# Decode attention beside a gated MLP: K and V loaded by 32 pairs of batch and head and 4 key blocks, in rows of 32 KB

## The chip, the cores and the metric

The kernel runs on one core of one Trainium2 chip. The metric is the time of one execution in microseconds (us), as the device counts it. Three runs of the kernel before took 365.57, 366.02 and 365.81 us; the median is 365.81 us. The profile is of one execution more, with its own span.

## The reference

```python
def _A_ref(x, k_cache, v_cache, wq, wo):        # x 8x1x576, caches 8x16x8192x128
    W = min(4096, max(256, Sk // 4))            # 2048: only the last 2048 keys count
    q = (x @ wq) in 32 heads of 128             # wq 576x4096, two query heads for each K/V head
    scores = q @ k[last W].T * (Dh ** -0.5)
    o = softmax(scores) @ v[last W]
    return o (8 x 4096) @ wo                    # wo 4096x576

def _B_ref(x, w1, b1, w2, b2):
    h = gelu(layernorm(x) @ w1 + b1)            # w1 576x4608
    return h @ w2 + b2                          # w2 4608x576

g = sigmoid((x * gate_w).sum(-1))
out = g * a + (1 - g) * b
```

There are 8 batches of one token each. K and V of the last 2048 keys are 8 x 16 x 2048 x 128 bf16 values each, 67 MB each; with the weights the kernel reads 154 MB once.

## The kernel before

**How the order comes about.** Every piece of work is an op with an engine, a cost, a priority and dependences (`_Plan.add`, `_Plan.dma`). `schedule` (line 62) is a greedy list scheduler: it takes the ready op with the smallest start time less 0.2 us times its priority. What it gives is a fixed order for each engine, and `emit` (line 141) writes the ops in that order with semaphore waits. So an engine never passes an op that waits. The big loads all go out on SyncE's queue (SP), in the order of a list named `stream` (line 571), and each load waits until its slot in SBUF is free.

**The start.** x and the gate come in on ScalarE's queue; wq (4.6 MB) and w1 (5.2 MB) come first on SP's. VectorE makes the layer norm, TensorE the query projection (`q_fn`, line 489) and the first MLP product (`h_fn`, line 524). ScalarE and VectorE make the gelu.

**K and V.** `load_item` (line 600) loads K or V of one K/V head for all 8 batches: 4 MB, as 256 rows of 64 keys by 128 values, that is 16 KB, two rows in each of 128 partitions. There are four slots of 4 MB and a half one. The stream is K0 K1 K2, then V and K in turn, a chunk of wo after every fourth V, and at the end the bias and w2.

**Scores** (`k_unit`, line 639). VectorE transposes K in blocks of 32 x 32 pairs of bf16, half of a load's 2 x 2 pieces at a time (line 647, 128 x 2048 f32), into one of two halves of the tile KT. TensorE then multiplies eight times (line 659, and line 175 for those that keep the weights of the one before), 512 columns each, with a block-diagonal query tile qbd. The results add up in PSUM banks 0 to 3 over the four units of a group of two K/V heads, on top of a mask that ScalarE wrote there (line 629): in each of the 128 rows of scores a quarter of the 2048 columns is that row's batch, and the rest is masked by -1e9.

**Softmax** (line 617), once for each of 8 groups: VectorE takes the maximum over 2048 columns (line 620), a small matmul (line 622) combines the four quarters, ScalarE writes the exponential with its sum (line 624) into the tile P, VectorE transposes P as a whole into PT (line 631), and a small matmul (line 633) gathers the sums.

**The product with V** (`v_item`, line 671). 32 matmuls for each V load (line 681): the weights are 128 x 32 pieces of PT, the moving side is 512 columns of V, in four column positions of the array. At a group's end VectorE picks the valid quarter and sums (lines 691 and 694), GpSimd and TensorE sort it (lines 696 and 700), ScalarE scales it by the gate (line 703) and VectorE transposes it into oT (line 706).

**wo, w2 and the end.** `AccGroup` (line 554) adds products into bank 7, two matmuls of 288 columns for each block of 128 rows (line 563). A wo chunk of 8 blocks is used right after the two groups that it belongs to. After the last V come the bias and w2 in pieces of 12, 12, 8, 3 and 1 blocks. Then two casts (lines 777 and 778) and two stores (line 780).

## Time and profile before

| | before |
|---|---|
| median of 3 runs | 365.81 us (365.57 to 366.02) |
| the profiled execution: span | 364.9 us |
| moved, mean rate over the span | 154.47 MB, 423 GB/s |
| K and V loads | 32 of 4096 KB |
| busy: PE, DVE, ACT, POOL | 247.1, 217.0, 39.9, 23.3 us |
| mean granted TensorE clock | 0.846 |

The profiled execution has no time of its own beside its span; the runs lie 0.7 to 1.1 us above it. The span is counted from the first to the last instruction. PE is TensorE's matmuls, PEld its weight loads, DVE VectorE, ACT ScalarE, POOL GpSimd and SP SyncE. A matmul's row has the duration of one matmul with its drain, and matmuls overlap, so rates are read from the starts. In an answer by windows, each row has the window, its length, the busy time of each engine with the number of instructions, then the granted TensorE clock, the share of the DMA engines and the rate in GB/s. In a timeline, the columns are start, duration, engine, line, operation, output and input, and the count; brackets hold the idle time ahead and what ended it.

### The profile page before, as it was taken

What the parts mean: (1) busy time and instruction counts of PE and PEld (TensorE: products, weight loads), DVE (VectorE), ACT (ScalarE), POOL (GpSimd) and SP (SyncE); (2) the same over time, 40 slices, a digit from 0 to 9 for tenths busy, and PEclk for the clock granted to TensorE, in tenths of its full rate; (3) what the DMA queues carried; (4) which work ended last, traced back from release to release, by engine and by line L of the source; (5) the groups of instructions that cost most, each with busy time, mean ns of one, the idle gap of its engine ahead of it and who ended that gap; (6) DMA issues with size and microseconds to landing.
All of it is one profiled execution on the core that took longest, in us unless ns stands there. A gap on an engine that the chain in (4) does not pass through costs nothing.

```text
span 364.9 us, 2626 instructions
## 1 busy us (share of the span) xinstructions
PE 247.1 (68%) x1347; PEld 57.3 (16%) x893; DVE 217.0 (59%) x160; ACT 39.9 (11%) x46; POOL 23.3 (6%) x66
## 2 busy tenths in 40 slices
PE   0355676599486957849297957868396938587776
PEld 0100000122111121202111121202110210102333
DVE  0723999667883757256675657276756667085220
ACT  1012100400310040000400040000400040001100
POOL 7210001000100000001000100001000100000000
PEclk9986599699769986969768986989589968969699
DMA  8999999999999999999999999999999999999996
GB/s 347 432 408 429 431 433 427 408 429 432 429 431 431 436 427 431 433 431 433 428 431 433 424 433 429 431 435 431 433 429 433 433 431 429 431 431 431 426 428 263
DMA packets 10674, 154.47 MB, mean 423 GB/s; under 512 B 764, under 2 KB 932, under 8 KB 1320
## 3 DMA queue, kind: packets, MB, share of 16 engines
q1 hardware_dynamic: 10608, 154.29, 99.1%
q8 instruction: 8, 0.13, 0.1%
q10 hardware_dynamic: 56, 0.03, 0.0%
q14 instruction: 2, 0.02, 0.0%
HBM read 154.31 MB, written 0.01 MB: 423 GB/s over the span
## 4 chain that ended last, share of the span: by engine, by line
DMA 66%; DVE 21%; PE 10%; issue 1%; ACT 1%; SPq 0%; DVEq 0%
DMA arena<-in_A_k_cache_dram 59%; DVE arena L647 20%; DMA arena<-in_B_w_dram 7%; PE ps L175 5%; PE ps L659 2%; PE ps L681 2%; DVE arena L546 1%; DVE arena L620 1%; ACT ps L629 1%; PE ps L563 0%; DVE arena L545 0%; PE ps L633 0%; DVE arena L777 0%; PE ps L622 0%; SPq L406 0%
## 5 line engine op out<-in xcount | busy, mean ns | idle before, releaser
L647 DVE STREAM_TRANSPOSE arena<-arena 128x2048 f32<-128x2048 f32 x64 | 144.1, 2289 | 61.8 <-DMA arena<-in_A_k_cache_dram 40.6
L175 PE MATMUL ps<-arena 128*128 128x512 bf16 (+2 forms) x454 | 135.0, 449 | 0.0
L659 PE MATMUL ps<-arena 128*128 128x512 bf16 x128 | 57.7, 451 | 52.5 <-DVE arena L647 52.5
L681 PE MATMUL ps<-arena 128*32 128x512 bf16 x512 | 60.3, 390 | 2.6 <-DVE arena L635 1.9
L624 ACT ACTIVATE arena<-ps,arena 128x2048 bf16<-128x2048 f32 x8 | 15.7, 1967 | 240.5 <-DVE arena L623 240.5
L659 PEld LDWEIGHTS ps<-arena 128*128 128x128 bf16 x128 | 14.0, 109 | 171.9 <-DVE arena L647 114.6
L681 PEld LDWEIGHTS ps<-arena 128*32 128x32 bf16 x512 | 25.2, 99 | 46.1 <-issue 20.3
L620 DVE TENSOR_REDUCE arena<-ps 128x1 f32<-128x2048 f32 x8 | 18.3, 2287 | 12.5 <-PE ps L175 12.4
L614 POOL COPY arena<-arena 32x128 bf16<-32x128 bf16 x32 | 9.2, 288 | 211.3 <-PE ps L175 201.5
L631 DVE STREAM_TRANSPOSE arena<-arena 128x2048 bf16<-128x2048 bf16 x8 | 18.3, 2292 | 6.4 <-ACT arena L624 6.4
L691 DVE SCALAR_TENSOR_TENSOR arena<-ps,arena 128x512 f32<-128x512 f32 x8 | 6.0, 751 | 19.8 <-PE ps L681 19.8
L563 PE MATMUL ps<-arena 128*8 128x288 bf16 (+1 forms) x140 | 12.6, 339 | 6.9 <-DVE arena L706 5.6
L700 PE MATMUL ps<-arena 128*128 128x256 f32 x16 | 5.8, 444 | 16.0 <-POOL arena L696 16.0
L633 PE MATMUL ps<-arena 128*128 128x1 f32 x16 | 4.6, 359 | 15.0 <-ACT ps L629 14.2
L629 ACT ACTIVATE ps<-arena 128x2048 f32<-128x2048 f32 x7 | 13.1, 1876 | 0.1
L696 POOL TENSOR_TENSOR arena<-arena 128x256 f32<-128x256 f32 x8 | 4.9, 612 | 111.3 <-DVE arena L623 63.3
L438 PE MATMUL ps<-arena 8*128 8x8 bf16 x8 | 0.6, 171 | 14.7 <-DVE arena L412 9.6
L694 DVE TENSOR_REDUCE arena<-arena 128x128 f32<-128x512 f32 x8 | 8.4, 1048 | 0.3
L563 PEld LDWEIGHTS ps<-arena 128*8 128x8 bf16 (+1 forms) x140 | 6.4, 97 | 13.5 <-DVE arena L706 7.0
L703 ACT ACTIVATE arena<-ps,arena 64x256 bf16<-64x256 f32 x8 | 3.7, 465 | 43.1 <-PE ps L700 43.1
L706 DVE STREAM_TRANSPOSE arena<-arena 128x256 bf16<-128x256 bf16 x4 | 2.5, 634 | 9.8 <-ACT arena L703 9.8
L541 DVE TENSOR_TENSOR arena<-arena 128x1152 f32<-128x1152 f32 x1 | 1.4, 1359 | 10.5 <-ACT arena L539 10.5
(88 smaller groups left out, 66.2 us busy)
## 6 DMA issues: line engine op xcount, KB each, us to landing
arena<-in_A_k_cache_dram SPq DMA_DIRECT2D x16, 4096.0 KB, 28.1
arena<-in_A_v_cache_dram SPq DMA_DIRECT2D x16, 4096.0 KB, 33.0
arena<-in_B_w_dram SPq DMA_DIRECT2D x1, 4608.0 KB, 23.4
arena<-in_A_wo_dram SPq DMA_DIRECT2D x4, 1152.0 KB, 34.7
arena<-in_A_wq_dram SPq DMA_DIRECT2D x1, 4096.0 KB, 13.0
arena<-in_B_w_dram SPq DMA_DIRECT2D x2, 1728.0 KB, 27.3
arena<-in_B_w_dram SPq DMA_DIRECT2D x1, 1152.0 KB, 26.7
arena<-in_B_w_dram SPq DMA_DIRECT2D x1, 576.0 KB, 24.3
```

Source lines behind the costliest of these rows:

```text
L175: return e.add_instruction(mybir.InstMatmult(name=nc.get_next_instruction_name(), engine=mybir.EngineType.PE, ins=[e.lower_ap(rhs), e.lowe ...
L563: ins = e.matmul(ps[32 * j:32 * j + 8, BK_ACC, 0:JN], lhsT, rhs[:, JN * j:JN * j + JN], start=False, stop=True, skip_group_check=True, til ...
L614: return e.tensor_copy(dst, src)
L620: mx = add("dve", lambda e: e.tensor_reduce(out=k(MX), in_=ps[:, 0:4, :].rearrange("p a n -> p (a n)"), axis=AXL.X, op=ALU.max), deps=[qk_ ...
L624: ex = add("act", lambda e: e.activation(out=Pm, in_=ps[:, 0:4, :].rearrange("p a n -> p (a n)"), func=ACTF.Exp, bias=k(NB), scale=SCALE, ...
L629: mask_done[g + 1] = add("act", lambda e: e.activation(out=ps[:, 0:4, :].rearrange("p a (n c) -> p (a n) c", c=4), in_=bass.AP(arena_f, of ...
L631: pt_done[g] = add("dve", lambda e: e.transpose(bass.AP(arena, offset=aoffs("PT") + 2048 * (g % 2), ap=[[AST, 128], [8, 64], [512, 4], [1, ...
L647: tr = add("dve", (lambda h=h, kb=kb: lambda e: e.transpose(bass.AP(arena_f, offset=foffs("KT") + kb * 2048, ap=[[AST // 2, 128], [1, 2048]]),
L659: mm = e.matmul(*args, start=False, stop=True, skip_group_check=True) if rc == 0 else held_matmul(nc, e, *args, stop=True, skip=True)
L681: mm = e.matmul(ps[c:c + 32, BK_OS[g % 2], :], PT[:, g % 2, 16 * c + 32 * t:16 * c + 32 * t + 32], slot(s)[:, (j % 2) * SE + 512 * t:(j % ...
L691: vmul = add("dve", lambda e: e.scalar_tensor_tensor(out=vmv, in0=ps[:, BK_OS[g % 2], :].rearrange("p (r d) -> p r d", r=4), scalar=rr[:, ...
L694: acc_ev[g] = add("dve", lambda e: e.tensor_reduce(out=EV[:, g % 2, :], in_=vm.rearrange("p (r d) -> p d r", r=4), axis=AXL.X, op=ALU.add) ...
```

## The change

A load of K or V now takes 32 pairs of batch and K/V head (two batches) by a quarter of the keys (512): 128 rows, one for each partition, of 128 keys by 128 values, that is 32 KB. There are 4 groups of two batches (NG), and 4 turns of one K and one V load in each (NT), 16 turns in all (NU). The stream is K0 K1 V0 K2 V1 ..., K15 V14 V15, then w2's first 24 blocks, wo in two chunks of 16 blocks, the bias, and w2's last 12.

- **Scores.** As before there are four transposes and 32 matmuls for a K load. Every turn has its own softmax now, 16 instead of 8. The mask leaves one column of eight.
- **Softmax.** The maximum is taken row by row, with no matmul, and the exponential uses it. At a group's end `group_weights` makes from the four maxima and sums of each row the weights by which the four turns are put together.
- **P.** The exponentials are written pair by pair in another order. Four transposes of 32 partitions (`sp`) lay the first half of P into a block-diagonal tile BD, a fifth (`pc`) turns the second half into the tile PC, and ScalarE lays that into BD with four copies of 32 partitions (`sq`). BD is set to zero once, by GpSimd; there is one, so that the spreading of a turn waits for the V product of the turn before (`later`). The last turn uses KT's space instead, which GpSimd sets to zero after the last score.
- **The product with V.** 64 matmuls for each V load, in two halves of 32, each with its own weights of 128 x 128 (every second element of BD's row) and 256 moving columns. VectorE adds the results, weighted, into the tile X, eight operations in a group; two more split X into two bf16 parts, 16 matmuls with the selectors seld sort it, and one VectorE operation scales it into oT.
- **wo** is multiplied after the last group, since every row of it needs all groups.

```diff
-        HG = 2
-        NG = Hkv // HG
+        NB_ = 2
+        NG = B // NB_
+        NT = 4
+        NK = W // (4 * NT)
...
-        WOR = 8
+        WOR = 16
+        WOP = Hq * Dh // 128
...
-        def load_item(cache, nm, hkv):
+        def load_item(which, nm, t):
             s = take_slot()
-            src = cache[:, hkv, S0:Sk, :].rearrange("b (x r) d -> x b (r d)", x=32)
+            g, xq = divmod(t, NT)
+            k0 = S0 + 4 * NK * xq
+            src = ck[which][32 * g:32 * g + 32, k0:k0 + 4 * NK, :].rearrange("i (x r) d -> i x (r d)", x=4)
...
+        def softmax(t):
+            g, x = divmod(t, NT)
+            scores = ps[:, 0:4, :].rearrange("p a n -> p (a n)")
+            mx = add("dve", lambda e: e.tensor_reduce(out=k(g, MX + x), in_=scores, axis=AXL.X, op=ALU.max), deps=[qk_unit[t]], name="mx%d" % t, cost=2.29, prio=5)
+            nb = add("dve", lambda e: e.tensor_scalar(out=k(g, NB + x), in0=k(g, MX + x), scalar1=-SCALE, ...
+            ex = add("act", lambda e: e.activation(out=bass.AP(arena, offset=aoffs("P"), ap=[[AST, 128], [64, 32], [1, 2], [2, 32]]),
+                                                   in_=ps[:, 0:4, :].rearrange("p a (r e c) -> p (a r) e c", e=2, c=32), func=ACTF.Exp, bias=k(g, NB + x), scale=SCALE, accum_out=k(g, S + x)),
+                     deps=[nb] + (p_read[t - 1] if t else [o_zz]), name="exp%d" % t, cost=2.2, prio=5)
...
+            if t + 1 < NU:
+                mask(t + 1, [ex])
...
+            dp = [ex] + bd_zero[home]
+            for a in range(4):
+                def fn(e, a=a):
+                    return e.transpose(bass.AP(arena_f, offset=32 * a * (AST // 2) + foffs(home) + 32 * a, ap=[[AST // 2, 32], [128, 16], [1, 32]]),
+                                       bass.AP(arena_f, offset=32 * a * (AST // 2) + foffs("P"), ap=[[AST // 2, 32], [1, 512]]))
+                sp_done[t][0].append(add("dve", fn, deps=dp, name="sp%d_%d" % (t, a), cost=0.65, prio=5))
+            pc = add("dve", lambda e: e.transpose(view("PC").bitcast(F32), bass.AP(arena_f, offset=foffs("P") + 512, ap=[[AST // 2, 128], [1, 512]])),
+                     deps=[ex] + (sp_done[t - 1][1] if t else []), name="pc%d" % t, cost=0.65, prio=5)
+            for a in range(4):
+                def fn(e, a=a):
+                    return e.activation(out=bass.AP(arena, offset=32 * a * AST + aoffs(home) + 64 * a + 4096, ap=[[AST, 32], [256, 16], [1, 64]]),
+                                        in_=bass.AP(arena, offset=32 * a * AST + aoffs("PC"), ap=[[AST, 32], [64, 16], [1, 64]]), func=ACTF.Copy)
+                sp_done[t][1].append(add("act", fn, deps=[pc] + bd_zero[home], name="sq%d_%d" % (t, a), cost=1.15, prio=3))
+            if x == NT - 1:
+                group_weights(g)
...
+            for v in range(2):
+                def pv_fn(e, v=v):
+                    mm = None
+                    for n in range(NK // 4 * v, NK // 4 * (v + 1)):
+                        q, ee = divmod(n, 2)
+                        mm = e.matmul(dst, bass.AP(arena, offset=aoffs(home) + 256 * q + ee, ap=[[AST, 128], [2, 128]]),
+                                      slot(s).rearrange("p (r k d) -> p r k d", r=2, d=128)[:, :, n, :], start=(n == 0), stop=(n == NK // 2 - 1), skip_group_check=True)
+                    return mm
+                pv = add("pe", pv_fn, deps=[d] + sp_done[t][v] + ([x_read[g - 1]] if g else [o_u]), name="pv%d_%d" % (t, v), cost=4.1, after=pe_hist[-1:])
...
-        M_CUTS = [[12, 12], [8, 3, 1]]
-        stream += [("B", 0)] + [("M", i) for i in range(len(M_CUTS))]
+        M_CUTS = [[24], [8, 3, 1]]
+        stream += [("M", 0), ("W", 0), ("W", 1), ("B", 0), ("M", 1)]
...
+        for t, v, pv in later:
+            for o in sp_done[t][v]:
+                o.deps.append(pv)
```

`group_weights` makes, for each group, small VectorE operations on 1 to 8 columns (`m1`, `mq`, `nm`, `ws`, `ss`, `w8`, `sb`, `rc`, `rg`), one small exponential and two small matmuls; the accumulations into X are named `x`, the split `xh` and `xl`, the sorting `sx` and the scaling `oT`.

In the built program VectorE's fixed order, from the second group on, is this, with `mx` for the maximum and `tr` for a transpose of K. After the `mx` of a group's second turn: `nb`, `tr`, `sp` x4, `pc`, `tr` x3. After that of the third: `nb`, `sp` x4, `pc`, `tr` x4. After that of the fourth: `nb`, `m1`, `mq`, `sp` x4, `pc`, `nm`, `tr` x3, `ws`, `w8`, `x` x4, `ss`, `tr`, `sb`. After that of the next group's first: `nb`, `rc`, `rg`, `tr`, `sp` x4, `pc`, `x` x4, `xh`, `xl`, `tr`, `oT`, `tr` x2. TensorE's order in a turn is four times eight score matmuls, then the two halves of the V product of the turn; after the V product of a group's last turn come two of the next score halves and then `sx`.

## The prediction

> **What bounds the kernel now.** I read the page's slices first, then its chain, then a long window of the loads, then the end of the chain in order of time.
>
> ```profile
> span 364.9 us, 2626 instructions
> ...
> DMA  8999999999999999999999999999999999999996
> GB/s 347 432 408 429 431 433 427 408 429 432 429 431 431 436 427 431 433 431 433 428 431 433 424 433 429 431 435 431 433 429 433 433 431 429 431 431 431 426 428 263
> ...
> DMA 66%; DVE 21%; PE 10%; issue 1%; ACT 1%; SPq 0%; DVEq 0%
> ...
> arena<-in_A_k_cache_dram SPq DMA_DIRECT2D x16, 4096.0 KB, 28.1
> ```
> ```profile
> 40.00:340.00 300.00, 214.68 (x1054) 45.87 (x669) 197.56 (x121) 32.34 (x30) 12.35 (x35) 0.84 1.01 430
> ```
> ```profile
> 334.54 26.68 DMA arena<-in_B_w_dram
> 361.22 0.04 issue
> 361.26 1.73 PE ps L563 x24
> 362.99 0.02 issue
> 363.01 0.45 DVE arena L777
> ```
>
> The DMA engines are full in every slice but the first and last, and the rate stays near 430 GB/s. A K load lands 28.1 us after its issue, although 4096 KB (4.19 MB) at 430 GB/s take 9.75 us: about three loads always stand in the queue. So the loads set the end, and the compute only follows; after the last landing at 361.22 come 3.7 us. What the change does to the time depends on two things: the rate of the loads, and whether the new compute of a turn stays under the 19.5 us that its two loads take.
>
> **The loads.** K and V are 134.2 MB. The second slice holds only wq and w1, whose rows are 32 and 36 KB, at 432 GB/s; K and V at 16 KB run at 430. If 32 KB rows go at 432, they save 134.2/0.430 - 134.2/0.432 = 1.4 us; wo's and w2's longer rows (the slices of 426 and 428) some 0.2 more. No row has 32 KB rows of K, so the bounds are the highest and lowest slice of K and V: at 436 it would be 4.3 us saved, at 408 16.8 us lost. I take 1.6, nearest to the row of like size. Were the loads still the limit, the span would be 363.3 us. The median 365.81 lies 0.9 above the profiled span, so the time would be 364.2.
>
> **The compute of a turn.** These rows price it.
>
> ```profile
> L620 DVE TENSOR_REDUCE arena<-ps 128x1 f32<-128x2048 f32 x8 | 18.3, 2287 | 12.5 <-PE ps L175 12.4
> L631 DVE STREAM_TRANSPOSE arena<-arena 128x2048 bf16<-128x2048 bf16 x8 | 18.3, 2292 | 6.4 <-ACT arena L624 6.4
> L504 DVE STREAM_TRANSPOSE arena<-arena 128x1024 bf16<-128x1024 bf16 x1 | 1.2, 1245 | 0.0
> L624 ACT ACTIVATE arena<-ps,arena 128x2048 bf16<-128x2048 f32 x8 | 15.7, 1967 | 240.5 <-DVE arena L623 240.5
> L624 ACT ACTIVATION_READ_ACCUMULATOR arena<-ps,arena 128x1 f32 x8 | 1.5, 193 | 0.0
> L544 ACT ACTIVATE arena<-arena 128x1152 f32<-128x1152 f32 x1 | 1.2, 1163 | 2.3 <-DVE arena L543 2.3
> L691 DVE SCALAR_TENSOR_TENSOR arena<-ps,arena 128x512 f32<-128x512 f32 x8 | 6.0, 751 | 19.8 <-PE ps L681 19.8
> L541 DVE TENSOR_TENSOR arena<-arena 128x1152 f32<-128x1152 f32 x1 | 1.4, 1359 | 10.5 <-ACT arena L539 10.5
> L420 DVE TENSOR_TENSOR arena<-arena 8x576 f32<-8x576 f32 x1 | 0.7, 747 | 0.0
> L621 DVE TENSOR_SCALAR arena<-arena 128x4 f32<-128x4 f32 x8 | 1.8, 231 | 0.3
> L510 PEld LDWEIGHTS ps<-arena 128*128 128x128 bf16 x4 | 0.3, 98 | 4.0 <-DVE arena L504 3.9
> ```
> ```profile
> 23.18 0.33 PEld L510 LDWEIGHTS ps<-arena 128*128 128x128 bf16 x4 [3.93 <-DVE arena L504]
> 23.19 0.61 PE L510 MATMUL ps<-arena 128*128 128x256 bf16 x4 [2.60 <-DVE arena L504]
> ...
> 276.76 8.89 DVE L647 STREAM_TRANSPOSE arena<-arena 128x2048 f32<-128x2048 f32 x4 [5.69 <-DMA arena<-in_A_k_cache_dram]
> 279.13 0.40 PE L659 MATMUL ps<-arena 128*128 128x512 bf16 x1 [2.76 <-DVE arena L647]
> ...
> 280.04 0.39 PE L659 MATMUL ps<-arena 128*128 128x512 bf16 x1
> ...
> 301.56 0.61 PE L659 MATMUL ps<-arena 128*128 128x512 bf16 x1 [2.47 <-DVE arena L647]
> ...
> 303.25 0.63 PE L659 MATMUL ps<-arena 128*128 128x512 bf16 x1
> ...
> 361.26 1.71 PE L563 MATMUL ps<-arena 128*8 128x288 bf16 x24 [1.11 <-DMA arena<-in_B_w_dram]
> ```
>
> - Transposes of K: 8.89/4 = 2.22 us each. A half of scores, eight matmuls: from 279.13 to 280.04 are four, so 1.82 us, and 0.17 more until its results count (0.40 less 0.23). At the lower clock, 301.56 to 303.25, it is 3.4 us.
> - Maximum 2.29; `nb` 0.2, by the 0.23 of line 621; exponential and its sum 1.97 + 0.19, some 2.1.
> - `sp` and `pc`, five transposes of 512: lines 631 and 504 give 1.02 ns an element and 0.2 us fixed, so 0.72, or 0.65 where they overlap as K's do. I take 0.70, 3.5 us a turn; 32 partitions cost no less than 128 as far as a row shows.
> - `sq`: 1024 elements against 1152 in 1.16 us, so 4.1 us for four. It is on ScalarE beside the first half of the V product and is not in the ring below.
> - The V product: line 510 is nearest, four matmuls of 256 columns, each with its own 128 x 128 weights. Its 0.61 us less one duration of 0.275 is three steps, 0.112 each; 64 make 7.2 us. If the weight loads (0.33/4, 0.08 each) were not hidden, 0.19 each, 12.2 us.
> - The additions `x`, 128 wide: 0.75 us less 384 elements at 1.06 ns (lines 541 and 420) is 0.34.
>
> Where the old kernel could run a group's scores ahead of its softmax, a turn's softmax now stands in a ring with VectorE and TensorE: last half of scores 2.0, maximum 2.3, `nb` 0.2, exponential 2.1, `sp` and `pc` 3.5, then the transposes of the next K. By the built order, after the second turn's maximum one transpose lies beside the exponential and three follow `pc`: 10.1 + 6.7 = 16.8 us. After the third, all four follow: 10.1 + 8.9 = 19.0. After the fourth, four, four `x` and five small operations: 21.3. After the next first, three, four `x`, `xh`, `xl`, `oT` and a wait for `sx`: about 19.6. Together 76.7 us for four turns; their loads at 432 GB/s take 77.7. **At full clock the compute just fits, by 1 us in 78.**
>
> **The clock.** Does TensorE keep it? These windows lie on the steps of the granted clock.
>
> ```profile
> 273.85:277.26 3.41, 2.52 (x14) 0.29 (x4) 0.50 (x1) 0.00 (x0) 0.00 (x0) 1.00 1.02 437
> 277.26:280.67 3.41, 1.54 (x7) 0.19 (x2) 3.41 (x2) 0.00 (x0) 0.00 (x0) 1.00 1.04 447
> ...
> 290.91:294.32 3.41, 1.10 (x8) 0.59 (x4) 1.86 (x3) 1.10 (x1) 0.61 (x1) 1.00 1.05 452
> 294.32:297.73 3.41, 1.61 (x14) 0.71 (x14) 1.93 (x2) 3.31 (x4) 0.00 (x0) 0.50 0.99 423
> 297.73:301.14 3.41, 1.36 (x10) 0.68 (x6) 2.91 (x3) 0.00 (x0) 0.00 (x0) 0.50 1.00 428
> 301.14:304.56 3.42, 3.00 (x8) 0.28 (x3) 2.56 (x2) 0.00 (x0) 0.00 (x0) 0.50 0.99 426
> 304.56:307.97 3.41, 2.81 (x13) 0.27 (x3) 3.00 (x2) 0.00 (x0) 0.00 (x0) 1.00 1.01 428
> ```
>
> A window with 1.54 us of matmuls is followed by full clock, one with 1.10 by half; the clock comes back after a window that is nearly full (3.00). So a step of 3.41 us with over about 2 us idle costs the clock for one or two steps. In the new ring the V product follows the last half of scores and ends 7.2 us on. The first transpose of the next K ends, where it follows `pc`, after 0.2 + 2.3 + 0.2 + 2.1 + 3.5 + 2.2 = 10.5. So TensorE idles 3.3 us after the third turn's scores and some 2.9 after the fourth's (a small matmul stands between); elsewhere the gaps are 1.5 us and less. A gap of 3.1 us has over 2.1 in one step in about 7 of 10 positions. Two such gaps, and a small chance at `sx`, make 1.5 slow spells a group. A spell loses 1.7 us of matmuls for one step, 3.4 for two, less 0.8 that the halves have to spare beside the transposes (2 x 0.4): 0.9 to 2.6, I take 1.75. That is 2.6 us a group, less the margin of 1.0: the compute falls behind by 1.6 us a group, 6.4 in four, and about 2 in the first turns, where the gelu and the slow clock delay it. Before, such spells fell into the wait for K and cost nothing.
>
> **Where the lag shows.** Not in the loads: they are issued two to three ahead, so 8 us of lag empty no queue. It shows at the end, since wo needs every group. Behind K15 come V14, V15, 24 blocks of w2, wo and 12 blocks of w2, 18.4 MB, 42.7 us. The last turn's chain is four transposes 8.9, 2.0, 2.3, 0.2, 2.1, 3.5, `sq` 4.1, half a V product 3.8, two `x` and the split 1.4, `sx` and `oT` 1.7, so 30; w2 matmuls ahead of `sx` add 2.5 and wo 64 x 0.071 = 4.6 us: 37. The transposes of K15 themselves stand behind `sp` and `pc`, some 3 us. That leaves 2.5 us. Of 8.4 us of lag 5.9 are exposed: 363.3 + 5.9 = 369.2 span, **370.0 us**. The other parts cost nothing at this place: GpSimd's zeroing of KT (4096 elements of 4 bytes) lies beside the last maximum and exponential, the mask on ScalarE ends before the first new half can start, and the 16 masks and exponentials with `sq` fill ScalarE to under 9 of 19.4 us. If GpSimd's zeroing were late, each us would add one at the end.
>
> **Rivals.**
> 1. *The clock holds, or its spells cost less than the margin.* Then the loads stay the limit and the time is 364.2, faster than before. For it: the sum fits without spells, and the gap of 2.76 us ahead of 279.13 cost no clock. It decides where the idle part of one step stays under 2 us, or where spells take less than 1.0 us a group and 2.5 at the end. Also here: if longer rows gain nothing, 365.8. The Trainium skill (TensorE: Matmul & The Clock Gate, Part 1) lets the clock fall after an idle window of about 3.4 us; by that rule gaps of 3.3 would mostly keep it. The trace speaks against that rule, since the step from 290.91 was a third busy and the next had half clock.
> 2. *The weight loads of the V product are not hidden.* They are 128 wide now and read every second element. At 12.2 us the next scores start behind the V product, and the ring is 12.2 + 4 x 1.82 + 0.8, about 20.3 us a turn, 14 us more than the loads in 16 turns; less the 2.5 and with no slow spells, 376. Against it: line 510.
> 3. *The new addresses are slower.* Neighbouring rows of a load lay side by side in a batch; now each four do, and the next pair is 2 MB on. Priced by the slice of 408: 364.9 + 16.8 + 0.9 = 382.6, and then the compute has time to spare. No row of before speaks for it. The Trainium skill (DMA: Bandwidth & Descriptors, Latency and other measured facts) reports 207 instead of 214 GB/s for rows 512 KiB apart, 164 at 2 MiB and 103 at 4 MiB. An estimate from its mildest pair, 207/214, would be 10.6 us more; no run here shows it yet.
>
> **How the numbers follow.** The forecast has 0.47; by the bounds of `sp` (0.65 to 0.75, 1 us a group each way), of the spells and of the exposed end, its own range is 366 to 377. Rival 1 has 0.35, rival 2 0.10, rival 3 0.08. About 0.2%, 0.7 us, is what a measurement of this kernel can tell from no change; 365.1 to 366.5 holds 0.04 of rival 1 and 0.03 of the forecast. So faster 0.31, same 0.07, slower 0.62. The range 363.0 to 378.0 leaves out rival 3 and the edges of the others.
>
> **What would show it.** The rate of the slices with K and V near 432 (loads right) or below 425 (rival 3). Starts of the V product's matmuls 0.11 us apart (or 0.19, rival 2). The five transposes near 0.7 us each. The granted clock at 0.5 in some steps behind the third and fourth turns' V products, and the first transpose of a K starting later and later behind its landing, by about 8 us at K15 (if it stays under 4, rival 1). The chain's end on `sx`, `oT` and wo's matmuls instead of a w2 load. I would be wrong if the chain still ends in a load, or if VectorE's transposes wait for K in every turn.

## The result, and the profile after

The changed kernel takes 383.89 us (median of 4 runs, 383.47 to 384.52), beside 365.87 us for the kernel before on the same chip: 1.0495 times as long, 95% interval 1.048 to 1.051. The sign of the forecast was right and its size was not: 370.0 us was said, 13.9 us too little, and the time lies above the range. Of one experiment below (the extra transpose in the held order) three of four runs took 399.76 to 401.66 us at a lower granted clock (0.885 to 0.889 beside 0.913) and are left out, so that a single run of it is used.

The page of the changed kernel, the lines that answer to those of before:

```profile
span 383.0 us, 3868 instructions
...
PEclk9966796989996999996998889898979999898999
...
GB/s 334 469 411 436 435 428 425 421 435 430 438 433 438 438 436 435 429 419 431 435 431 419 405 376 364 431 438 433 404 435 306 421 421 423 421 433 431 411 180 4
...
DVE 51%; PE 24%; ACT 12%; DMA 9%; issue 3%; SPq 0%
...
arena<-in_A_k_cache_dram SPq DMA_DIRECT2D x16, 4096.0 KB, 16.9
```

The chain of work that ended last was 66% loads; now it is 51% VectorE, 24% TensorE and 12% ScalarE. The loads no longer set the end: their rate drops to 376, 364 and 306 GB/s in three slices, the last two hold 180 and 4, and a K load lands 16.9 us after its issue instead of 28.1, so the queue is shorter. The end of the chain, in order of time, is what the forecast said it would be: the last turn's `sq` and V product, then w2, `sx`, `oT` and wo.

```profile
365.82 1.06 ACT arena L654
...
366.92 3.67 PE ps L730 x32
370.59 2.06 PE ps L563 x32
...
374.57 0.45 DVE arena L769
...
375.07 6.01 PE ps L563 x92
```

Next I read what VectorE waited for (the engine and line that wait, what they wait for, us in all, times, longest), since a ring that is late shows as waits on VectorE for the other engines and none for a load.

```profile
DVE arena L629 <- PE ps L175: 31.4, 15, 2.5
DVE arena L646 <- ACT arena L632: 19.7, 16, 2.7
DVE arena L693 <- PE ps L175: 14.9, 13, 2.0
```

That is the ring of the prediction: the maximum waits for the last half of scores, the first `sp` for the exponential, the transposes of K for scores that must free a half of KT. No line here waits for K's load. Then the pieces themselves, by line and form:

```profile
L632 ACT ACTIVATE arena<-ps,arena 128x2048 bf16<-128x2048 f32 x16 | 40.8, 2548 | 158.0 <-DVE arena L630 158.0
...
L632 ACT ACTIVATION_READ_ACCUMULATOR arena<-ps,arena 128x1 f32 x16 | 2.9, 183 | 0.0
```
```profile
L693 DVE STREAM_TRANSPOSE arena<-arena 128x2048 f32<-128x2048 f32 x64 | 145.6, 2296 | 15.0 <-PE ps L175 14.9
L646 DVE STREAM_TRANSPOSE arena<-arena 32x512 f32<-32x512 f32 x64 | 45.0, 703 | 21.2 <-ACT arena L632 19.7
...
L649 DVE STREAM_TRANSPOSE arena<-arena 128x512 f32<-128x512 f32 x16 | 11.4, 711 | 0.5
```

One piece is plainly not what I priced: the exponential has 2048 elements a row as before and takes 2548 ns instead of 1967. A turn in which no transpose of K lies beside it (the third of the second group), from the timeline:

```profile
169.00 0.15 DVE L630 TENSOR_SCALAR arena<-arena 128x1 f32<-128x1 f32 x1
169.19 2.54 ACT L632 ACTIVATE arena<-ps,arena 128x2048 bf16<-128x2048 f32 x1 [6.84 <-DVE arena L630]
171.61 0.18 ACT L632 ACTIVATION_READ_ACCUMULATOR arena<-ps,arena 128x1 f32 x1
...
171.81 2.90 DVE L646 STREAM_TRANSPOSE arena<-arena 32x512 f32<-32x512 f32 x4 [2.66 <-ACT arena L632]
174.75 0.71 DVE L649 STREAM_TRANSPOSE arena<-arena 128x512 f32<-128x512 f32 x1
175.39 4.46 DVE L693 STREAM_TRANSPOSE arena<-arena 128x2048 f32<-128x2048 f32 x2
```

VectorE stands still for 2.66 us, from the end of `nb` to 171.81. The exponential with its sum is 171.81 - 169.19 = 2.62 us on the path, and `sp` and `pc` are 175.39 - 171.81 = 3.58. TensorE's clock in the steps around this turn (window, its length, busy time of PE, PEld, DVE, ACT, POOL, then clock, share of DMA, GB/s):

```profile
169.29:172.70 3.41, 3.41 (x33) 3.04 (x32) 0.85 (x2) 3.38 (x3) 0.00 (x0) 1.00 1.05 447
172.70:176.11 3.41, 0.93 (x9) 0.58 (x6) 3.32 (x5) 1.61 (x2) 0.00 (x0) 0.99 1.02 442
176.11:179.53 3.42, 1.41 (x4) 0.25 (x2) 3.42 (x2) 3.35 (x4) 0.00 (x0) 0.50 0.91 393
179.53:182.94 3.41, 3.41 (x10) 0.29 (x2) 1.92 (x2) 0.26 (x1) 0.00 (x0) 0.51 1.00 432
```

The step behind the V product has 0.93 us of matmuls, and the two after it run at half clock, in which the next scores fall: the gap that the forecast described, at its place.

### The profile page after: what moved, and what is told of

Same layout as the page of the kernel before. It is cut to its first block, busy times and chain, and to the rows that moved or that the text cites. A ratio compares the mean times of both kernels' runs of the same rounds, so it can differ in the third digit from the quotient of the medians.

```text
span 383.0 us, 3868 instructions
## 1 busy us (share of the span) xinstructions
PE 281.6 (74%) x1864; PEld 127.1 (33%) x1404; DVE 273.9 (72%) x295; ACT 146.9 (38%) x126; POOL 20.5 (5%) x50
## 4 chain that ended last, share of the span: by engine, by line
DVE 51%; PE 24%; ACT 12%; DMA 9%; issue 3%; SPq 0%
DVE arena L693 23%; PE ps L175 15%; DVE arena L646 11%; ACT arena L632 11%; DVE arena L629 10%; DMA arena<-in_A_k_cache_dram 9%; PE ps L706 5%; DVE arena L649 3%; PE ps L563 2%; DVE arena L745 2%; ACT arena L654 1%; PE ps L730 1%; DVE arena L630 1%; DVE arena L546 1%; ACT ps L661 0%
## 5 line engine op out<-in xcount | busy, mean ns | idle before, releaser
L175 PE MATMUL ps<-arena 128*128 128x512 bf16 (+3 forms) x475 | 135.1, 435 | 37.1 <-DVE arena L693 34.1
L693 DVE STREAM_TRANSPOSE arena<-arena 128x2048 f32<-128x2048 f32 x64 | 145.6, 2296 | 15.0 <-PE ps L175 14.9
L730 PE MATMUL ps<-arena 128*128 128x256 bf16 x1024 | 116.1, 274 | 2.0 <-ACT arena L654 1.3
L730 PEld LDWEIGHTS ps<-arena 128*128 128x128 bf16 x1024 | 100.6, 99 | 25.4 <-issue 10.6
L632 ACT ACTIVATE arena<-ps,arena 128x2048 bf16<-128x2048 f32 x16 | 40.8, 2548 | 158.0 <-DVE arena L630 158.0
L654 ACT ACTIVATE arena<-arena 32x1024 bf16<-32x1024 bf16 x64 | 67.5, 1054 | 31.9 <-DVE arena L649 21.6
L706 PEld LDWEIGHTS ps<-arena 128*128 128x128 bf16 x128 | 13.6, 106 | 185.8 <-DVE arena L693 116.2
L646 DVE STREAM_TRANSPOSE arena<-arena 32x512 f32<-32x512 f32 x64 | 45.0, 703 | 21.2 <-ACT arena L632 19.7
L629 DVE TENSOR_REDUCE arena<-ps 128x1 f32<-128x2048 f32 x16 | 36.6, 2289 | 31.4 <-PE ps L175 31.4
L661 ACT ACTIVATE ps<-arena 128x2048 f32<-128x2048 f32 x16 | 30.1, 1882 | 0.5
L649 DVE STREAM_TRANSPOSE arena<-arena 128x512 f32<-128x512 f32 x16 | 11.4, 711 | 0.5
L432 PE MATMUL ps<-arena 8*128 8x8 bf16 x8 | 0.6, 170 | 14.6 <-DVE arena L405 9.5
L745 DVE SCALAR_TENSOR_TENSOR arena<-ps,arena 128x128 f32<-128x128 f32 x28 | 9.7, 346 | 1.6 <-PE ps L730 0.7
L541 DVE TENSOR_TENSOR arena<-arena 128x1152 f32<-128x1152 f32 x1 | 1.4, 1359 | 11.1 <-ACT arena L539 11.1
L826 ACT ACTIVATE arena<-ps 8x288 bf16<-8x288 f32 x1 | 0.4, 401 | 13.9 <-PE ps L563 13.9
## 6 DMA issues: line engine op xcount, KB each, us to landing
arena<-in_A_k_cache_dram SPq DMA_DIRECT2D x16, 4096.0 KB, 16.9
arena<-in_A_wq_dram SPq DMA_DIRECT2D x1, 4096.0 KB, 12.8
```

What stands on the lines that cost most here:

```text
L175: return e.add_instruction(mybir.InstMatmult(name=nc.get_next_instruction_name(), engine=mybir.EngineType.PE, ins=[e.lower_ap(rhs), e.lowe ...
L629: mx = add("dve", lambda e: e.tensor_reduce(out=k(g, MX + x), in_=scores, axis=AXL.X, op=ALU.max), deps=[qk_unit[t]], name="mx%d" % t, cos ...
L632: ex = add("act", lambda e: e.activation(out=bass.AP(arena, offset=aoffs("P"), ap=[[AST, 128], [64, 32], [1, 2], [2, 32]]), in_=ps[:, 0:4, ...
L646: return e.transpose(bass.AP(arena_f, offset=32 * a * (AST // 2) + foffs(home) + 32 * a, ap=[[AST // 2, 32], [128, 16], [1, 32]]), bass.AP ...
L649: pc = add("dve", lambda e: e.transpose(view("PC").bitcast(F32), bass.AP(arena_f, offset=foffs("P") + 512, ap=[[AST // 2, 128], [1, 512]]) ...
L654: return e.activation(out=bass.AP(arena, offset=32 * a * AST + aoffs(home) + 64 * a + 4096, ap=[[AST, 32], [256, 16], [1, 64]]), in_=bass. ...
```

## The experiments

My theory after the result was the ring of the prediction with pieces that are too long (**ring theory**): the exponential above all, then the clock. The rivals were that the new addresses slow the loads (**load theory**), and that the lost clock is nearly the whole of it (**clock theory**). Each time below stands beside the kernel before on the same chip (365.75 to 365.89 us).

**e1_dense: the exponential writes as before.**

```diff
-            ex = add("act", lambda e: e.activation(out=bass.AP(arena, offset=aoffs("P"), ap=[[AST, 128], [64, 32], [1, 2], [2, 32]]),
-                                                   in_=ps[:, 0:4, :].rearrange("p a (r e c) -> p (a r) e c", e=2, c=32), func=ACTF.Exp, ...
+            ex = add("act", lambda e: e.activation(out=Pm, in_=scores, func=ACTF.Exp, ...
```

> The exponential writes P in its natural order, as the kernel before did, instead of pair by pair into every second 2-byte element; the transposes and products then run over a P in another order, so the output is not the reference's. Ring theory (the turn's ring of softmax, transposes and scores sets the time, and its pieces were priced too low): the exponential goes from 2548 ns back to about 1967 ns, 0.58 us in each of 16 turns, 9.3 us at most, so about 375 us. Load theory (the new addresses are slow): no change, 384. Clock theory (the lost clock is nearly the whole miss and the exponential's length is covered): under 3 us, 381 to 384.

Measured: 372.81 us (370.15 to 374.97), ratio to before 1.019 (1.013 to 1.0249). That is 11.1 us less than the changed kernel, where the ring theory said at most 9.3 and each rival under 3. The difference of 1.8 is taken up with e19 below.

**e2_warm: unused matmuls behind each V product.**

```diff
+            if t < NU - 1:
+                keep_warm(t)
...
+        def keep_warm(t):
+            def fn(e):
+                mm = None
+                for n in range(24):
+                    args = (ps[:, BK_ACC, 288:512], zeros_bf, maskR[:, 0:224])
...
+            pe_hist.append(add("pe", fn, deps=[o_z, o_mR], name="warm%d" % t, cost=0.1, after=pe_hist[-1:], prio=9))
```

> After the V product of each turn but the last, TensorE does 24 more matmuls of 224 columns whose results are not used (2.2 us at full clock), so that its idle stretch stays about 1 us and the granted clock holds. Ring theory: a turn's pieces at full clock sum to 79.3 us a group against 82.6 measured, so 3.3 x 4 = 13 us less, about 371 us, and not less than that, because the longer pieces stay. Clock theory (the lost clock is the whole difference from the loads' limit): 364 to 366. Load theory: 384, no change.

Measured: 370.48 us (370.17 to 371.54), ratio 1.0133 (1.0117 to 1.0149): 13.4 us less, as the ring theory said. The page's clock row and VectorE's waits show where from:

```profile
PEclk9999696999999899999999999999999999999999
```
```profile
DVE arena L646 <- ACT arena L632: 19.7, 16, 2.7
```
```profile
L693 DVE STREAM_TRANSPOSE arena<-arena 128x2048 f32<-128x2048 f32 x64 | 144.6, 2291 | 2.6 <-PE ps L175 2.0
```

The clock holds, and the transposes' wait for scores falls from 14.9 to 2.0 us, which is the 13 us. The wait for the exponential is the same 19.7 us.

**e3_quarter: the loads alone.**

```diff
-            for r2 in range(2):
-                for h in range(2):
-                    n = 4 * t + 2 * r2 + h
+            for r2 in range(1):
+                for h in range(1):
+                    n = t
```

> Only one of a K load's four transposes and score halves is computed, three quarters of the scores are left out; all loads stay as they are. The compute of a turn is some 14 us then, far under the 19.5 us of its two loads, so this is the time of the loads with the new rows alone. Ring and clock theories: 363.5 to 365 us, and the slices near 432 GB/s. Load theory (the new addresses are slower): 375 to 383.

Measured: 367.17 us (365.88 to 367.66), ratio 1.0025 (1.0007 to 1.0044). The load theory falls. The rate between 40 and 340 us, and the end of the chain:

```profile
40.00:340.00 300.00, 187.04 (x1146) 117.34 (x1041) 150.99 (x203) 137.50 (x115) 8.86 (x10) 0.75 1.00 433
```
```profile
320.89 37.09 DMA arena<-in_A_wo_dram
...
358.03 5.71 PE ps L563 x60
```

433 GB/s, where it was 430 before. But the time is 3 us above the 364.2 that I gave to the loads' limit: wo's second half is among the last loads now, and 60 matmuls in 5.71 us follow it, at a granted clock of 0.51 from 358 to 361 us, where 24 in 1.73 us followed the last load before.

**e8_extra: one more transpose a turn.**

```diff
+            add("dve", lambda e: e.transpose(view("PC2").bitcast(F32), bass.AP(arena_f, offset=foffs("P"), ap=[[AST // 2, 128], [1, 512]])),
+                deps=[ex, pc], name="px%d" % t, cost=0.65, prio=5)
```

> One more 128x512 transpose of P (0.73 us) in VectorE's order in each of 16 turns, behind the one that is there, into a tile that nobody reads. Ring theory: each is exposed in full, 16 x 0.73 = 11.7 us, about 395 us (within 3 us, since slow spells can fall another way). Load theory: no change, 384. Clock theory: more than 12 us, if the longer idle stretch of TensorE (by 0.73 us) adds slow spells too, some 398 to 402.

Measured: 376.13 us (375.45 to 378.79), ratio 1.0296 (1.0258 to 1.0333): 8 us **faster** than the changed kernel, though VectorE does 16 transposes more. No theory had that. The profile says what moved:

```profile
L697 DVE STREAM_TRANSPOSE arena<-arena 128x2048 f32<-128x2048 f32 x64 | 145.1, 2292 | 8.7 <-PE ps L175 7.6 <-DMA arena<-in_A_k_cache_dram 1.1
L647 DVE STREAM_TRANSPOSE arena<-arena 32x512 f32<-32x512 f32 x64 | 45.0, 703 | 10.9 <-ACT arena L633 9.1
...
L658 DVE STREAM_TRANSPOSE arena<-arena 128x512 f32<-128x512 f32 x16 | 11.4, 711 | 0.5
```

The added row (line 658) costs its 11.4 us, but the wait for the exponential falls from 19.7 to 9.1 us and that for scores from 14.9 to 7.6. The longer turn changed the list scheduler's order: in the changed kernel six of 15 turns (3, 6, 7, 10, 11, 14) have no transpose of K beside the exponential, here one (7). So it was an experiment on the order, and not on the cost that it was meant for.

**e11_beside: that order alone** (the first transpose of the next K ahead of `sp` in every turn; the scheduler moves a few small operations with it).

```diff
+        for t in range(NU - 1):
+            for o in p_read[t]:
+                o.after.append(tr_hist[4 * t + 4])
```

> Nothing is added or left out; VectorE's order alone is changed: in each turn the first transpose of the next K comes ahead of the five transposes of P, so that it lies beside the exponential. In the changed kernel six of the 15 turns (3, 6, 7, 10, 11, 14) have no such transpose there, and VectorE stands idle while ScalarE makes the exponential. Ring theory: 2.3 us less in each of the six, 14 us, so the ring comes down to about 75 us a group, under the 77.5 us that its loads take at 433 GB/s, and the time goes to the loads' limit, which the run without most of the scores put at 367: 367 to 371 us. Clock theory (what is lost is lost to the clock, and the longer pieces of VectorE are covered): 378 to 384.

Measured: 369.34 us (368.69 to 369.9), ratio 1.0098 (1.0082 to 1.0113): 14.6 us less, with the same instructions. A fourth turn, from its timeline:

```profile
185.67 2.56 ACT L632 ACTIVATE arena<-ps,arena 128x2048 bf16<-128x2048 f32 x1 [6.84 <-DVE arena L630]
...
186.84 2.30 DVE L693 STREAM_TRANSPOSE arena<-arena 128x2048 f32<-128x2048 f32 x1
...
189.07 2.86 DVE L646 STREAM_TRANSPOSE arena<-arena 32x512 f32<-32x512 f32 x4
```

The transpose fills the time of the exponential, and `sp` follows it at once. VectorE's wait for the exponential is 6.9 us in all instead of 19.7.

```profile
DVE arena L646 <- ACT arena L632: 6.9, 13, 1.6
```

**e12_extra_order: the extra transpose, the order held.**

```diff
+        by = {o.name: o for o in P.all if o.eng == "dve"}
+        ch = ("tr0_00 tr0_01 tr0_10 tr0_11 tr1_00 mx0 nb0 tr1_01 sp0_0 sp0_1 sp0_2 sp0_3 pc0 px0 " \
...
+        for a_, b_ in zip(ch, ch[1:]):
+            by[b_].after.append(by[a_])
```

> The extra 128x512 transpose of P again, but with the rest of VectorE's order held as in the changed kernel, turn for turn. Ring theory: each of the 16 is exposed in full, 16 x 0.73 = 11.7 us, about 395 us (393 to 399 as slow spells fall). If instead an extra transpose of this kind really costs nothing or helps, as the 376 us of the run with another order could be read: 376 to 384.

Measured: 391.75 us in the run that is used, the shortest of the four and 7.9 us more than the changed kernel. So the extra transpose does cost time where the order is held, and the reading that it is free falls; but 7.9 is two thirds of the 11.7 that the ring theory said, and with one run the share of it that is exposed stays open.

**e4_dense_warm: both gains together** (the edits of e1 and e2).

> The dense exponential and the 24 unused matmuls together (P in another order, so the output is not the reference's). Ring theory: 79.3 us a group at full clock less 4 x 0.58 is 77.0, just under the loads' 77.5 us, so the loads' limit, 366 to 368 us. If the two gains do not add because they take away the same idle stretch: 369 to 371.

Measured: 369.0 us (366.87 to 369.58), ratio 1.0078 (1.0048 to 1.0109). Alone the two give 11.1 and 13.4 us; together 14.9. In e4's profile VectorE begins to wait for loads:

```profile
L692 DVE STREAM_TRANSPOSE arena<-arena 128x2048 f32<-128x2048 f32 x64 | 144.6, 2290 | 5.9 <-PE ps L175 5.1 <-DMA arena<-in_A_k_cache_dram 0.7
```

0.7 us of waiting for K is little: the ring is now about as long as the loads. The median lies at the lower edge of the second answer (369 to 371) and one of the four runs in the first (366 to 368), so the time does not tell which holds: whether the gains share the same idle stretch or the loads' limit cuts them off stays open.

**e7_both: the scores' columns in another order, and P spread by ScalarE.**

```diff
-                                rhs = bass.AP(arena, offset=aoffs("KT") + kb * 4096 + rc * 1024 + ee, ap=[[AST, 128], [2, 512]])
+                                rhs = bass.AP(arena, offset=aoffs("KT") + kb * 4096 + rc * 1024 + ee, ap=[[AST, 128], [128, 8], [2, 32], [64, 2]])
...
-                sp_done[t][0].append(add("dve", fn, deps=dp, name="sp%d_%d" % (t, a), cost=0.65, prio=5))
-            pc = add("dve", lambda e: e.transpose(view("PC").bitcast(F32), bass.AP(arena_f, offset=foffs("P") + 512, ap=[[AST // 2, 128], [1, 512]])),
+            pc = add("dve", lambda e: e.transpose(view("PC").bitcast(F32), bass.AP(arena_f, offset=foffs("P"), ap=[[AST // 2, 128], [1, 1024]])),
...
+            for v in range(2):
+                for a in range(4):
...
+                    sp_done[t][v].append(add("act", fn, deps=[pc] + bd_zero[home], name="sq%d_%d%d" % (t, v, a), cost=1.07, prio=3))
```

> The scores' columns come out in such an order (the moving side of the score matmuls reads KT in another order, the mask follows) that the exponential is written densely; and the whole of P is turned by one transpose of 128x1024, with all eight copies into BD on ScalarE. So VectorE's part of the ring falls by the four 32-partition transposes less the longer one, some 2.4 us a turn, and the exponential by 0.58. Ring theory: about 70 us a group, far below the loads, so the loads' limit with its end, 366 to 368 us. If the ScalarE copies (8 x 1.05 us a turn) become a new wait of the V product: 372 to 380.

Measured: 478.48 us (477.91 to 478.87), ratio 1.3081 (1.3061 to 1.31). Neither answer. The exponential is short (1968 ns) and the copies are not late; the scores are:

```profile
179.51 0.70 PE L701 MATMUL ps<-arena 128*128 128x512 bf16 x1
180.05 1.77 PE L175 MATMUL ps<-arena 128*128 128x512 bf16 x3
181.66 0.70 PE L701 MATMUL ps<-arena 128*128 128x512 bf16 x1
182.19 1.77 PE L175 MATMUL ps<-arena 128*128 128x512 bf16 x3
```

Starts at 179.51, 180.05, 181.66 and 182.19: 0.54 us from one score matmul to the next, where the kernel before had 0.23 (279.13 to 280.04 for four). 512 of them add 0.31 x 512 = 159 us to TensorE, which sets the turn now. The moving side is read here in pieces of one bf16, 128 bytes apart, where it had been every second element.

**e19_gather: the order changed in the exponential's reading instead.**

```diff
-            ex = add("act", lambda e: e.activation(out=bass.AP(arena, offset=aoffs("P"), ap=[[AST, 128], [64, 32], [1, 2], [2, 32]]),
-                                                   in_=ps[:, 0:4, :].rearrange("p a (r e c) -> p (a r) e c", e=2, c=32), ...
+            ex = add("act", lambda e: e.activation(out=Pm.rearrange("p (n c e) -> p n c e", c=32, e=2),
+                                                   in_=ps[:, 0:4, :].rearrange("p a (r e c) -> p (a r) c e", e=2, c=32), ...
```

> Nothing is left out: the exponential goes through the scores in the order in which P lies, so that it writes P densely and reads the scores in PSUM 128 bytes apart; P is the same as in the changed kernel. Ring theory, if only the scattered writing made it slow: 1.97 us instead of 2.55 and the time of the run with the dense exponential, 370 to 375 us. If reading in that order costs as much as writing did: 2.55 us, 384. (Reading KT in a scattered order cost TensorE 0.54 instead of 0.23 us a matmul in the run before, so this isn't free of doubt.)

Measured: 373.23 us (372.21 to 374.41), ratio 1.0205 (1.018 to 1.023), as e1, with the whole computation done.

```profile
L632 ACT ACTIVATE arena<-ps,arena 128x2048 bf16<-128x2048 f32 x16 | 31.5, 1968 | 156.2 <-DVE arena L630 156.2
```
```profile
L693 DVE STREAM_TRANSPOSE arena<-arena 128x2048 f32<-128x2048 f32 x64 | 144.9, 2292 | 10.2 <-PE ps L175 9.6 <-DMA arena<-in_A_k_cache_dram 0.6
L646 DVE STREAM_TRANSPOSE arena<-arena 32x512 f32<-32x512 f32 x64 | 44.7, 699 | 14.3 <-ACT arena L632 12.8
```

So the scattered writing is what costs, and reading the scores in PSUM 128 bytes apart is free. Why more than 16 x 0.58 = 9.3 us are gained is explained only in part. The wait for the exponential falls by 6.9 us (19.7 to 12.8) and not by 9.3, because in nine turns of the changed kernel a transpose of K lies beside it and `sp` waited only 0.2 to 0.5 us. The transposes' wait for scores falls too (14.9 to 9.6), while that of the maximum grows (31.4 to 35.1). These rows give 8.5 us together, and the rest of the 10.7 stays open; the granted clock is 0.922 where it was 0.902.

**e20_best: dense, beside, and wo ahead of w2** (the edit of e19, that of e11 with the small wait `nm` behind `pc`, and this):

```diff
-        stream += [("M", 0), ("W", 0), ("W", 1), ("B", 0), ("M", 1)]
+        stream += [("W", 0), ("W", 1), ("B", 0), ("M", 0), ("M", 1)]
```

> Nothing is left out. Three edits together: the exponential written densely as in the run beside this one, one transpose of the next K ahead of P's transposes in every turn (and the small wait for the combined maximum behind them), and wo loaded ahead of w2's 24 blocks, so that w2's small pieces and not wo end the stream. Ring theory: 79.3 us a group less 4 x 0.58 and less 6 x 2.3 / 4 is 73.5, 4 us under the loads' 77.5, so the loads are the limit; they end near 360.4 as in the run without most of the scores, with 3.7 us behind them as in the kernel before: span 364.1, time 364.5 to 365.5 us, as fast as the kernel before or 0.3% faster. If the clock still holds the ring above the loads: 367 to 369. If the exponential stays at 2.55 us: 75.8 a group and 365 to 367.

Measured: 367.67 us (367.2 to 368.54), ratio 1.0061 (1.0047 to 1.0075): not the 364.5 to 365.5 of the full gain. The number lies in the 367 to 369 that were said for a clock that holds the ring above the loads, but the cause is another. The timeline shows that the ring is done with, since K15's first transpose waits for its load, and the chain shows what is late instead.

```profile
319.48 2.31 DVE L693 STREAM_TRANSPOSE arena<-arena 128x2048 f32<-128x2048 f32 x1 [0.81 <-DMA arena<-in_A_k_cache_dram]
```
```profile
353.07 0.45 DVE arena L769
...
353.57 10.19 PE ps L563 x136
```

136 matmuls of wo and w2 stand behind the last `oT`, in 10.19 us.

**e24_best_m16: 16 of w2's blocks ahead of V15** (with e20's exponential and order of VectorE; w2's matmuls are also kept behind the V products that come before them).

```diff
-        M_CUTS = [[24], [8, 3, 1]]
-        stream += [("M", 0), ("W", 0), ("W", 1), ("B", 0), ("M", 1)]
+        M_CUTS = [[16], [8], [8, 3, 1]]
+        stream.insert(stream.index(("V", NU - 1)), ("M", 0))
+        stream += [("W", 0), ("W", 1), ("B", 0), ("M", 1), ("M", 2)]
```

> Nothing is left out. The dense exponential and the transposes beside it as in the run with the three edits, where K15's first transpose waited for K15's load (no lag left) and the end was 136 matmuls of w2 and wo in 10.2 us behind the last sorting. Here 16 of w2's 24 blocks are loaded ahead of V15 and their 32 matmuls stand ahead of V15's product, so that 108 are left behind the sorting. Theory that only those matmuls were in the way: they end at about 353.6 + 108 x 0.075 = 361.7, as early as the last pieces of w2 land, so the loads are the limit at both ends: span 364.4, time 365.6 to 366.0, the same as the kernel before. If the last turn's chain is what is late, and not the matmuls behind it: 367 to 368, no gain.

Measured: 367.46 us (366.07 to 368.82, 12 runs), ratio 1.0042 (1.0026 to 1.0058). The median lies in the 367 to 368 of the second answer, but the runs lie in two heaps, five from 366.07 to 366.69 and seven from 367.17 to 368.82, and neither answer is shown. The profiled run is of the upper heap:

```profile
334.04 21.35 DMA arena<-in_B_b_dram
...
355.43 9.98 PE ps L563 x108
```
```profile
355.38:358.80 3.42, 3.37 (x28) 1.64 (x30) 0.00 (x0) 0.00 (x0) 0.00 (x0) 0.50 0.99 418
```

There the four matmuls of the bias, which stand ahead of wo's in TensorE's order, waited for the bias's load until 355.38, the clock fell to 0.50 meanwhile, and 108 matmuls took 9.98 us instead of the 8.1 that were expected. Whether the lower heap is the same kernel without that fall stays open: the mean clocks of the two (0.911 to 0.930, and 0.907 to 0.925) overlap. (The profiles of e3 and of e9 below differ by just such a fall.)

**e9_rows16 and e25_rows16b: rows of 16 KB** on top of e3. In e9 the transfer was written with the row in two parts:

```diff
-            src = ck[which][32 * g:32 * g + 32, k0:k0 + 4 * NK, :].rearrange("i (x r) d -> i x (r d)", x=4)
+            src = ck[which][32 * g:32 * g + 32, k0:k0 + 4 * NK, :].rearrange("i (x u r) d -> i x u (r d)", x=4, u=2)
```

> As the run without three quarters of the scores, but each K and V row of 32 KB is moved as two of 16 KB, with the addresses as in the changed kernel. If the longer rows are what raised the rate from 430 to 433 GB/s: 430 or 431 between 40 and 340 us and 1.5 to 2.5 us more than with the long rows, 368.5 to 369.5. If the rows' length does nothing: 433 and 367.

Measured: 366.52 us (365.82 to 367.13), ratio 1.0018 (1.0007 to 1.0028), but the page's row of packets shows that the parts went as rows of 32 KB again (6150 packets, as in e3), so e9 is only e3 once more. Its ten runs lie in two heaps (365.82 to 366.12 and 366.92 to 367.13), and its profiled run, of the lower one, does not end as e3's did:

```profile
337.90 22.75 DMA arena<-in_B_w_dram
...
360.69 1.74 PE ps L563 x24
```

Here the clock stays at 1.00 behind wo's landing, and w2's last load sets the end, as before the change. The span is 364.4 us and e3's 365.7: the same instructions with a slow spell at the end took 1.3 us more.

In e25 each load is two transfers of 128 rows of 16 KB.

```diff
+            for u in range(2):
+                d = dma("sp", lambda e, u=u: e.dma_start(slot(s).rearrange("p (u n) -> p u n", u=2)[:, u, :], src.rearrange("i x (u n) -> i x u n", u=2)[:, :, u, :]), ...
```

> As the run without three quarters of the scores, with each K and V load issued as two transfers of 128 rows of 16 KB, so that the rows are really short (in the run meant for that they went as 32 KB again, 6150 packets as before). If the longer rows raised the rate from 430 to 433 GB/s: 430 or 431 between 40 and 340 us, and 1.5 to 2.2 us more than 366 to 367, so 367.5 to 369.5. If they do nothing: 433 GB/s and 366 to 367. If the neighbouring rows 2 MB on cost something that the long rows make up for: under 429 GB/s.

Measured: 369.1 us (367.97 to 369.1), ratio 1.0076 (1.0058 to 1.0093), with 10758 packets:

```profile
40.00:340.00 300.00, 188.07 (x1129) 115.52 (x1025) 151.15 (x200) 137.56 (x115) 8.86 (x10) 0.76 1.01 431
```

431 GB/s and 1.9 to 2.6 us more than e3 and e9. So the long rows save about 2 us and the addresses cost nothing. e25 also has twice as many transfers, which no run separates from the length of the rows; the kernel before, with rows of 16 KB in single transfers of 4 MB, ran at 430 GB/s.

No version that does the whole work beats the kernel before: the best runs, the lower heap of e24, come to 366.1 to 366.7 us beside 365.89. The change removes at most 2 us of loads and gives them back at the end, where wo must wait for the last group.

## Why the forecast was too low, step by step

**The loads: right.** 1.6 us were said for the longer rows. e25 takes 1.9 to 2.6 more than e3 and e9, the chain has wo's second half landing at 359.45 in it and at 357.98 in e3, 1.5 later, and the rate is 433 where 432 was said. Rival 3 falls by e3; that its 382.6 us lies near the measured time is chance. The Trainium skill (DMA: Bandwidth & Descriptors, Latency and other measured facts) has a loss for rows far apart by powers of two. At 433 GB/s, with each four rows side by side and the next four 2 MB on, the trace shows no such loss. The time at the loads' limit was wrong by 2 to 3 us (364.2 said for rival 1, 366.5 to 367.2 in e9 and e3). In e9's profile the last load lands at 360.65 and not at 359.6, and the time lies 1.5 us above the span where 0.9 was taken; e3's has the slow spell on wo's matmuls besides, since wo's second half is now one of the last loads.

**The ring: right in its shape, one piece mis-sized.** This is the step that failed: "Maximum 2.29; `nb` 0.2, by the 0.23 of line 621; exponential and its sum 1.97 + 0.19, some 2.1." The 1967 ns were of an exponential that wrote its row densely. The changed one writes every second bf16, and the forecast took the price without asking what the new order of the output does. It is 2.62 us on the path instead of 2.1: 16 x 0.52 = 8.3 us. With the dense writing, e20 has it at 1.97, 2.09 us to the next `sp`, just what was said, and e19 has 10.7 us less. `sp` and `pc` are 3.58 instead of 3.5, 16 x 0.08 = 1.3 us. By these two pieces a group would take 76.7 + 2.1 + 0.3 = 79.1 us at full clock. In e2, where the clock holds, the maxima of the first turns of the last three groups start at 126.88, 205.33 and 283.77, so it takes 78.45: other pieces were priced some 0.7 too high. Its loads take 77.5 at 433 GB/s. "At full clock the compute just fits, by 1 us in 78" was in truth 0.95 us too long.

**The clock: right in its mechanism, a little too cheap.** 2.6 us a group were said, 10.4 in all; taking the spells away (e2) saves 13.4. By the Trainium skill (TensorE: Matmul & The Clock Gate, Part 1) the clock falls after an idle window of about 3.4 us. That is too mild here as it was before: a step with 0.93 us of matmuls in 3.41 is followed by half clock. In e2, which fills those gaps, the clock holds and 13 us are gained. The rival "the clock holds" falls.

**The sum.** 8.3 for the exponential, 1.3 for `sp` and `pc`, 3.0 for the clock and 4 x 0.2 for the loads' shorter 77.5 are 13.4 of the 13.9 us by which the forecast was short. That this comes out so near is partly luck, as the start of the last turn's maximum shows. By the forecast's terms it would have been at 339.2: the last landing at 363.3 - 3.7 = 359.6, less 42.7 for K15's, then 8.4 of lag, 3 behind `sp` and `pc`, 8.9 of transposes and 2.0 of scores. The chains of the changed kernel and of e2 have it here:

```profile
353.76 2.30 DVE arena L629
```
```profile
340.76 2.30 DVE arena L629
```

It came 14.6 us late, and 0.7 of that was won back behind it (383.0 less 353.76 is 29.2 us to the end, where the forecast's terms have 29.9). The clock is 13.0 of the delay, 2.6 more than the 10.4 that were said. The other 12.0 are there with the clock held: 1.6 because K15 lands later than 359.6 less 42.7 (e3's chain waits for it until 318.53), and 10.4 of the ring. Of these, the 1.75 us a group that e2's maxima show (78.45 less 76.7) make 6.6 in the 15 turns ahead of the last. The other 3.8 must have arisen in the first turns, for which the forecast had "about 2"; what made them longer stays open. That the exponential's length costs time is shown by e1 and e19, and the clock's share by e2; `sp` and `pc` are read from the timeline alone. The shares are not independent: e1 and e2 together gain 14.9 and not 24.5.

**The lag and the loads: wrong.** "Not in the loads: they are issued two to three ahead, so 8 us of lag empty no queue" was said of 8 us; the lag at the last maximum was more than twice that (8.4 and 14.6 us), and the slices of 376, 364 and 306 GB/s show the queue run short. No run shows that this cost more: the chain behind K15 is of the ring and not of the loads.

**The V product: right.** 32 of its matmuls in 3.67 us are 0.11 each, and rival 2 falls.

**What I did not see: the order.** I read from the built order that six of the turns leave VectorE idle during the exponential, and counted it into the 19.0 and 21.3 us of two of the turns. But I took that order as given by the change. e11 shows that it is a choice of the list scheduler and worth 14.6 us, of the 17 that separate the changed kernel from the loads' limit (383.9 less 366.5 to 367.2).

## What to carry to other kernels

A duration from a row belongs to its access pattern as well as to its shape: before an operation is priced by an old row, compare the strides of what it reads and writes. Where work runs in a ring of engines, look at what an engine could do while it waits for another (here one transpose beside the exponential): the order of the same instructions was worth 14.6 of the 18.0 us that the change costs, and an experiment that adds an instruction can change that order, so hold the order or read it again. When a step is moved to the end of the stream, count its own work behind the last load.

## What the runs showed of the hardware

- ScalarE's exponential of 128 x 2048 took 2548 ns when it wrote bf16 with a step of 4 bytes, 1967 when it wrote densely, and 1968 when it wrote densely and read PSUM 128 bytes apart. The Trainium skill (ScalarE: Activation LUTs, What ACT_TABLE_LOAD costs) gives 1990 ns for such an operation of 2048 elements; the trace agrees for dense writing alone.
- A matmul of 512 moving columns started every 0.54 us instead of 0.23 when the moving side was read one bf16 at a time, 128 bytes apart; every second element had cost nothing, neither there (0.23 us for 512 columns is twice the 0.11 for the V product's 256, which lie densely) nor in the weights of the V product. The Trainium skill (Advanced Engine Details and Errata, SBUF Cachelines) asks for at least two accesses to each line of 16 bytes of SBUF. The score matmuls agree with it: four read one after the other from a line cost nothing, and one at a time from a line does. The exponential's writing, with four elements to a line, took 581 ns more (2548 less 1967), which that rule does not give.
- Two rows of 16 KB that lie side by side at both ends went as one of 32 KB (6150 packets in e9 as in e3, 10758 where they were issued apart).
